# Second MLP of a three-part kernel: its sums move from GpSimd to VectorE, products are chained in PSUM, stores are issued later

## The chip, the core and the metric

The kernel runs on one core of a Trainium2 chip. The metric is the device time of one execution in microseconds (us). A core has TensorE (PE in the profile; its weight loads are PEld), VectorE (DVE), ScalarE (ACT), GpSimd (POOL) and SyncE (SP), whose queue here issues nearly all DMA transfers. Each engine takes its instructions in order; semaphores tie the engines to one another.

## The reference

The computation has three parts in a row: an attention between 512 tokens and 32 state rows for 8 x 8 heads, a first MLP with a quadratic gate, and a second MLP with a leaky slope. Both MLPs take rows of 512 through 2048 channels back to 512.

```python
def _moe_ref(x, w_in, w_out):
    h = x @ w_in
    g = np.where(h >= 1, h, np.where(h <= -1, 0.0, (h + 1) ** 2 / 4))
    return g @ w_out

def _moe2_ref(x, w_in, w_out, alpha):
    h = x @ w_in
    g = np.maximum(h, 0.0) + alpha * np.minimum(h, 0.0)
    return g @ w_out

def reference(...):
    attn_out = _attn_ref(x, state)                 # (8, 8, 544, 64)
    x = attn_out.transpose(0, 2, 1, 3).reshape(4352, 512)
    x = _moe_ref(x, ...)
    return _moe2_ref(x, ...)                       # (4352, 512)
```

The weights come as 64-bit floats; the kernel decodes them on the chip.

## The kernel before

Every f32 operand of a product is split into a high half (fp32r, rounded by ScalarE: `hi_`, L73) and a low half, the difference (`lo_`, L76, a two-operand subtraction, on VectorE unless said otherwise). A product takes three matmuls: high x high, high x low, low x high.

*First MLP and attention* (0 to 723 us). Its steps are numbered by token block t and channel block f (`gi(t, f)`); the table `side` adds other work to a step: the weights of the second MLP are decoded there, w_in in about 255 to 453 us, w_out in 464 to 670 us. For w_out the sums that the second MLP needs are made at once: `w2_sums` on GpSimd, then `w2_put`, 56 of them (8 blocks of 256 channels x 7), each a high and a low half of 128 x 256 and a store to `w2d`. For w_in the decoded halves are stored to `wid` and loaded again later.

*Second MLP* (723 to 1441 us). It is a 2 x 2 block product done with seven products instead of eight, in both layers. The tokens are cut into five supersteps s, each with two halves of 448, 448, 448, 416, 416 columns. In a superstep:

- The first layer has 56 units `h_item`: for each weight block q (0 to 7) the products p in the order 0, 1, 3 (of the q before), 5, 2 (of the q before), 4, 6. A unit is six matmuls (L757) against the input halves xh, xl. Bank A collects p 0, 5, 6, 3, bank B p 1, bank E p 4 and 2. `h_after` makes the results: ScalarE copies the bank (p, u2, u3; L783, L788, L790), VectorE adds (`plus`, L779: c11, c22, c12), ScalarE takes the negative part m (L764) and VectorE multiplies it by alpha and adds (`slope`, L766). One result, m10, has no addition.
- `g_comb` (L805) combines the four results of a q for the products of the second layer: combination 3 in the first layer, 2, 4 and 1 in the first 24 units of the second layer. All are on GpSimd.
- The second layer has 56 units `o_item` (m = 8 i + k, product PO[i] in the order 0, 1, 5, 6, 4, 3, 2). A unit is six matmuls (L830), three for each half j of 256 output columns, into a bank accB for j. `o_split` makes the halves gs of a unit three units ahead. After k = 7 `o_after` copies product 0 (ScalarE) or adds (VectorE, L843), and `out_put` transposes (L867) into a tile ot and lists its stores, of 128-byte rows.
- Beside the second layer the inputs of the next superstep are combined and split (`x_comb`, L720; `x_split`, whose second low half xl is on GpSimd), every fourth unit from m = 10.
- Superstep 0 also makes the w_in sums in its first layer: `wr_get` loads, `w1_sums` (GpSimd), `w1_put` (halves and a store to `w1d`); it uses these tiles, later supersteps load wu from `w1d` (L738).

`second` writes all this in one order. Loads of weights (wu for the first layer, wv of 256 KB for the second, L743) are put on SP's queue six units ahead; before each unit one listed store (L887) is put on the same queue. Tiles of 128 x 512 come from the pool U, of 128 x 1024 (gs, inputs xr) from V; a tile is used again when its readers are done. A scheduler then fixes each engine's order when the program is built.

Of the kernel before, what the change touches and what calls it, by code (L numbers as in the profile page):

```python
# [34 lines left out]
ROWS = S + NS  # L35
# [5 lines left out]
def kernel_body(ctx: ExitStack, tc: tile.TileContext, x, state, w1i, w1o, w2i, w2o, alpha, out):  # L41
    nc = tc.nc
    up = ctx.enter_context(tc.tile_pool(name="up", bufs=80))
    vp = ctx.enter_context(tc.tile_pool(name="vp", bufs=10))
# [51 lines left out]
    wid = dp.tile([8, 2, 128, 512], F32, name="wid")  # L96
# [545 lines left out]
    def w2i_store(j, kh):  # L642
        ld.dma_start(out=wid[j, kh], in_=G.pop(("dec", ("w2i", j, kh))))

    def wr_get(q):

        for kh in range(2):
            t = U(f"wr{q}{kh}")
            ld.dma_start(out=t, in_=wid[q, kh])
            WR[q, kh] = t  # L650
# [7 lines left out]
    def four_sums(key, a11, a12, a21, a22, view):  # L658


        sa, sb = U(f"sa{key}"), U(f"sb{key}")
        s1, s2, s3, s4 = [view(t[:, h * 256:(h + 1) * 256]) for t in (sa, sb) for h in range(2)]
        for o, a, b, op in ((s1, a21, a22, ALU.add), (s2, s1, a11, ALU.subtract),
                            (s3, a11, a21, ALU.subtract), (s4, a12, s2, ALU.subtract)):
            pool.tensor_tensor(out=o, in0=a, in1=b, op=op)
        return {0: a11, 1: a12, 2: s4, 3: a22, 4: s1, 5: s2, 6: s3}

    def put(src, name, view, dst):
        t = U(name, F32R)
        h, l = t[:, :256], t[:, 256:]  # L670
        hi_(view(h), src)
        yield
        lo_(view(l), src, view(h))
        ld.dma_start(out=dst, in_=t.bitcast(F32))
        return t

    def w1_sums(q):
        r0, r1 = [parts(WR.pop((q, kh))) for kh in range(2)]
        WS[q] = four_sums(f"a{q}", r0[:, :, 0], r1[:, :, 0], r0[:, :, 1], r1[:, :, 1],
                          lambda t: t.rearrange("p (k c) -> p k c", k=2))  # L680

    def w1_put(q, *ps):
        for p in ps:
            t = yield from put(WS[q].pop(p), f"wu{q}{p}", lambda t: t.rearrange("p (k c) -> p k c", k=2), w1d[q, p])
            WU[0, q, p] = t
            yield

    def w2_sums(q):
        r0, r1 = [G.pop(("dec", ("w2o", 2 * q + e))) for e in range(2)]
        WS["o", q] = four_sums(f"o{q}", r0[:, :256], r1[:, :256], r0[:, 256:], r1[:, 256:], lambda t: t)  # L690

    def w2_put(q, *ps):
        for p in ps:
            yield from put(WS["o", q].pop(p), f"wo{q}{p}", lambda t: t, w2d[q, p])
# [26 lines left out]

    def x_split(s, p):
# [3 lines left out]
        for kk in range(2):  # L726
# [3 lines left out]
            lo_(l, r, h, pool if kk else dve)  # L730
# [37 lines left out]
    def h_after(s, q, p):  # L768
# [26 lines left out]
        elif p == 2:  # L795
            h = plus("c12", E, GT.pop((q, "u2")))
            slope(s, q, 0, 1, h, h)
            g_comb(q, 3)

    def g_comb(q, m):  # L800

        b11, b21, b12, b22 = [GR[q, e, tk] for tk in range(2) for e in range(2)]
        x, y, op = {3: (b22, b12, ALU.subtract), 2: (b12, b11, ALU.add),
                    4: (b21, b11, ALU.subtract), 1: (b22, b11, ALU.subtract)}[m]
        pool.tensor_tensor(out={3: b12, 2: b11, 4: b21, 1: b11}[m], in0=x, in1=y, op=op)  # L805

# [11 lines left out]
    def o_item(s, i, k):  # L818
        w = wof(s)
        p = PO[i]  # L820
        gh, gl = GS.pop((i, k))
        wt = WB.pop((s, i, k))
        wh, wl = wt[:, :256], wt[:, 256:]
        for j in range(2):
            if k == 0 and p != 2:
                OA["E" if p == 4 else p, j] = acc_ps(f"accB{s}{p}{j}")
            ps = OA["E" if p in (2, 4) else p, j][:, :w]
            js = slice(j * 128, (j + 1) * 128)
            for n, (a, b) in enumerate(((wh, gh), (wh, gl), (wl, gh))):
                pe.matmul(ps, a[:, js], b, start=(p != 2 and k == 0 and n == 0), stop=(k == 7 and n == 2),  # L830
                          skip_group_check=True)
        if k == 7:
            for j in range(2):
                o_after(s, p, j)

    def o_after(s, p, j):

        w = wof(s)
        ps = OA["E" if p in (2, 4) else p, j][:, :w]

        def plus(name, b):
            o = OC[name, j] = U(f"{name}{s}{j}")[:, :w]
# [3 lines left out]
        if p == 0:  # L846
            o = OC["p0", j] = U(f"op0{s}{j}")[:, :w]
            act.copy(o, ps)
        elif p == 1:
            out_put(s, 0, j, 0, plus("c11", OC["p0", j]))  # L850
        elif p == 5:
            plus("u2", OC.pop(("p0", j)))
        elif p == 6:
            plus("u3", OC["u2", j])
        elif p == 4:
            out_put(s, 1, j, 1, plus("c22", OC["u3", j]))
        elif p == 3:
            out_put(s, 1, j, 0, plus("c21", OC.pop(("u3", j))))
# [3 lines left out]
    def out_put(s, oh, j, tk, c):  # L862
# [3 lines left out]
        t = U(f"ot{s}{oh}{j}{tk}")[:, :w]  # L866
        dve.transpose(out=t, in_=c)  # L867
        g = 2 * oh + j
        c0, end = BASE[s] + tk * w, BASE[s] + (tk + 1) * w
        first = c0  # L870
        while c0 < end:
            b, r0 = divmod(c0, S)
            if b < NB:
                n = min(end, (b + 1) * S) - c0
                dst = out[b * ROWS + r0:b * ROWS + r0 + n, :].rearrange("(b i) (g j) -> g i b j", i=32, j=32)
            else:
                n = end - c0
                dst = out.rearrange("(b r) (g j) -> g r b j", r=ROWS, j=32)[:, S:, r0 // 32:(r0 + n) // 32]
            for a in range(4):
                src = t[32 * a:32 * a + 32, c0 - first:c0 - first + n].rearrange("p (b j) -> p b j", j=32)  # L880
                OS.append((dst[4 * g + a], src))
            c0 += n

    def out_store(n):
        for _ in range(min(n, len(OS))):
            dst, src = OS.pop(0)
            ld.dma_start(out=dst, in_=src)  # L887


    def second():  # L890
# [4 lines left out]
        for s in range(NSUP):  # L895
            os = [("o", s, i, k) for i in range(7) for k in range(8)]
            hs = [("h", s, q, p) for q, p in LS]
            ev += hs[:-2]
            ev += [os[0], os[1], hs[-2], os[2], os[3], hs[-1]] + os[4:]
        loads = [e for e in ev if e[0] == "o" or e[1]]  # L900
        nl = 0
        at_load = {e: n for n, e in enumerate(loads)}
        for n, (kind, s, a, b) in enumerate(ev):
            out_store(1)
# [235 lines left out]
```

## Time and profile before

| | us |
|---|---|
| runs, not profiled | 1458.29, 1454.10, 1453.76 (median 1454.1) |
| profiled execution | 1451.19 |
| its span, first to last instruction | 1449.4 |
| TensorE busy | 1390.5 (96%) |
| VectorE busy | 1082.6 (75%) |
| ScalarE busy | 841.7 (58%) |
| GpSimd busy | 352.9 (24%) |
| mean granted clock of TensorE | 0.987 of full |

Busy time says how long an engine had an instruction under way. Matmuls are pipelined, so several short gaps of TensorE don't show in its busy time; they show in the spacing of matmuls in a window. A row of a timeline gives in brackets how long the engine had been idle and what released it. The profile's lines are those of the listing above.

### The profile page before, as it was taken

The page shows a single profiled execution, that of the slowest core. Times are in us where ns is not written, and L with a number is a line of the kernel's source. Part 1 is how long each engine was busy: PE and PEld are TensorE (multiplying, and loading weights), DVE is VectorE, ACT ScalarE, POOL GpSimd, SP SyncE. Part 2 cuts the span into 40 slices and gives each one's busy share as a digit, 9 for nine tenths or more (in the row PEclk, how much of TensorE's full clock was granted, in tenths as well). Part 3 has the DMA queues.
Part 4 walks back from the last instruction along what each step waited for, and adds up shares of the span by engine and source line. Part 5 has one row for each costly group of instructions (what it writes and reads, how often), then busy time and mean ns, then how long its engine had stood idle before and what let it go on. Part 6 is the DMA issues. An engine that isn't in the chain of part 4 may idle for free. (4 is left out here: it accounts for less than half of the span.)

```text
span 1449.4 us, 20876 instructions
## 1 busy us (share of the span) xinstructions
PE 1390.5 (96%) x6596; PEld 1197.4 (83%) x6596; DVE 1082.6 (75%) x1765; ACT 841.7 (58%) x1628; POOL 352.9 (24%) x318
## 2 busy tenths in 40 slices
PE   6799999999999999999999899999999999899997
PEld 5466688888888888888987899888988899899987
DVE  6878685868787999784698884788477857885774
ACT  5566677777776777775565453445344434454542
POOL 1000001121100121110345820371136213711350
PEclk9999999999999999999999999999999999999999
DMA  5998316878744454677376479727983799389846
GB/s 198 310 311 301 118 51 159 226 220 231 218 136 141 153 190 167 208 235 236 139 256 230 145 249 297 251 97 229 286 278 114 222 281 317 118 254 280 303 118 177
DMA packets 267869, 306.01 MB, mean 211 GB/s; under 512 B 126704, under 2 KB 141040, under 8 KB 267760
## 3 DMA queue, kind: packets, MB, share of 16 engines
q1 hardware_dynamic: 228768, 287.13, 61.7%
q0 software_dynamic: 33280, 8.51, 3.2%
q10 hardware_dynamic: 5712, 9.05, 1.7%
q8 instruction: 53, 0.87, 0.2%
q14 instruction: 56, 0.46, 0.1%
HBM read 227.42 MB, written 76.55 MB: 210 GB/s over the span
## 5 line engine op out<-in xcount | busy, mean ns | idle before, releaser
L830 PE MATMUL accB<-gs,wv 128*128 128x448 f32 (+1 forms) x1680 | 347.8, 368 | 21.2 <-DMA wv<-w2d 13.7
L830 PEld LDWEIGHTS accB<-gs,wv 128*128 128x128 f32 x1680 | 322.2, 193 | 44.4 <-issue 14.3
L757 PE MATMUL hB<-xh,wu 128*128 128x448 f32 (+1 forms) x1120 | 323.5, 364 | 10.4 <-ACT u L788 4.5
L757 PEld LDWEIGHTS hB<-xh,wu 128*128 128x128 f32 x1120 | 210.7, 189 | 33.4 <-ACT u L788 6.3
L805 POOL TENSOR_TENSOR c<-c,c 128x448 f32<-128x448 f32 (+1 forms) x120 | 157.0, 1323 | 276.0 <-DVE c L766 188.0
L757 PE MATMUL hB<-xl,wu 128*128 128x448 f32 (+1 forms) x560 | 201.8, 360 | 0.0
L76 DVE TENSOR_TENSOR gs<-c,gs 128x448 fp32r<-128x448 f32 (+1 forms) x200 | 164.4, 851 | 29.3 <-ACT gs L73 28.2
L73 ACT CAST gs<-c 128x448 fp32r<-128x448 f32 (+1 forms) x200 | 109.7, 556 | 126.5 <-PE accB L830 99.2
L764 ACT ACTIVATE m<-c 128x448 f32<-128x448 f32 (+1 forms) x120 | 68.1, 568 | 120.7 <-DVE c L779 120.7
L766 DVE SCALAR_TENSOR_TENSOR c<-m,beta_sb,c 128x448 f32<-128x448 f32 (+1 forms) x120 | 90.5, 754 | 60.6 <-ACT m L764 60.0
L582 DVE SCALAR_TENSOR_TENSOR g<-y,hA 128x512 f32<-128x512 f32 (+1 forms) x144 | 94.0, 653 | 51.6 <-ACT y L580 51.1
L579 ACT ACTIVATE y<-hA 128x512 f32<-128x512 f32 (+1 forms) x144 | 82.5, 573 | 71.8 <-PE hA L84 71.7
L76 DVE TENSOR_TENSOR gl<-g,gh 128x512 fp32r<-128x512 f32 (+1 forms) x128 | 93.0, 726 | 35.1 <-ACT gh L73 33.1
L757 PEld LDWEIGHTS hB<-xl,wu 128*128 128x128 f32 x560 | 105.6, 189 | 5.0
L73 ACT CAST gh<-g 128x512 fp32r<-128x512 f32 (+1 forms) x128 | 75.7, 591 | 25.4 <-DVE g L582 23.9
L580 ACT ACTIVATE y<-y 128x512 f32<-128x512 f32 (+1 forms) x144 | 87.6, 608 | 4.3
L779 DVE TENSOR_TENSOR c<-hB,u 128x448 f32<-128x448 f32 (+1 forms) x80 | 48.5, 606 | 47.5 <-ACT u L790 41.3
L76 DVE TENSOR_TENSOR gs<-m,gs 128x448 fp32r<-128x448 f32 (+1 forms) x80 | 72.2, 920 | 12.6 <-ACT gs L73 11.6
L76 POOL TENSOR_TENSOR xl<-xr,xh 128x448 fp32r<-128x448 f32 (+1 forms) x35 | 41.9, 1201 | 162.9 <-ACT xh L73 148.1
L606 PE MATMUL accA<-g,wf_w1o 128*128 128x512 f32 x128 | 60.5, 605 | 4.6 <-DVE wf_w1o L399 4.6
L494 ACT COPY vgo<-vgp 128x512 f32<-128x512 f32 x64 | 37.3, 587 | 43.6 <-PE vgp L84 22.4
L113 POOL TENSOR_TENSOR bdf<-stT,mask 128x512 f32<-128x512 f32 x7 | 9.4, 1342 | 213.5 <-PE accA L614 108.6
(964 smaller groups left out, 2941.3 us busy)
## 6 DMA issues: line engine op xcount, KB each, us to landing
wv<-w2d SPq DMA_DIRECT2D x280, 256.0 KB
wu<-w1d SPq DMA_DIRECT2D x224, 256.0 KB
vd<-vgo SPq DMA_DIRECT2D x64, 256.0 KB
x<-in_x_dram SPq DMA_DIRECT2D x30, 512.0 KB
vr<-vd SPq DMA_DIRECT2D x56, 256.0 KB
w2d<-wo SPq DMA_DIRECT2D x56, 256.0 KB
w1d<-wu SPq DMA_DIRECT2D x56, 256.0 KB
wr_wi<-in_moe_w_in_dram SPq DMA_DIRECT2D x16, 512.0 KB
```

What stands on the lines that cost most here:

```text
L73: act.copy(h, raw)
L76: (eng or dve).tensor_tensor(out=l, in0=raw, in1=h.bitcast(F32), op=ALU.subtract)
L579: act.activation(out=y[:, :n], in_=ps, func=AF.Relu, bias=0.5, scale=0.5)
L580: act.activation(out=y[:, :n], in_=y[:, :n], func=AF.Square)
L582: dve.scalar_tensor_tensor(out=g[:, :n], in0=y[:, :n], scalar=1.0, in1=ps, op0=ALU.min, op1=ALU.max)
L606: pe.matmul(ACC[k], w[:, k * 128:(k + 1) * 128], g, start=(f == 0), stop=(f == NF - 1))
L757: pe.matmul(ps, a[:, kk], b, start=(new and m == 0), stop=(m == 5), skip_group_check=True)
L764: act.activation(out=m, in_=h, func=AF.Relu, scale=-1.0)
L766: dve.scalar_tensor_tensor(out=g, in0=m, scalar=beta_sb[:, f:f + 1], in1=h, op0=ALU.mult, op1=ALU.add)
L779: dve.tensor_tensor(out=o, in0=a, in1=b, op=ALU.add)
L805: pool.tensor_tensor(out={3: b12, 2: b11, 4: b21, 1: b11}[m], in0=x, in1=y, op=op)
L830: pe.matmul(ps, a[:, js], b, start=(p != 2 and k == 0 and n == 0), stop=(k == 7 and n == 2), skip_group_check=True)
```

## The change

The work on GpSimd in the second MLP goes to VectorE: combinations 3 and 2 right behind the first layer's results, combination 4 in the first layer for k 0 to 3 and at m 8 to 11 for the others, combination 1 at m 23 to 30 (now written to the third result's tile); and all xl. The halves of product 0 are made in the first layer, as are the first four of product 1; the others five units ahead. Products 0, 5, 6 and 3 are chained in one bank: the sums p0 + p5 and so on form in PSUM, ScalarE copies them where another product needs them, and p3 is transposed from PSUM. A unit of the second layer is now one j with two k. The last four units of a superstep alternate with the first four of the next. A tile ot (from V) holds both j, its rows in DRAM are 256 bytes, and a store is issued at least six units after it was listed, at the very end on SP's and ScalarE's queues in turn. The w_in sums are made in the first MLP's steps, right after decoding, and superstep 0 loads wu as the others do. Pool U has 72 tiles instead of 80, V 14 instead of 10.

```diff
-    up = ctx.enter_context(tc.tile_pool(name="up", bufs=80))
-    vp = ctx.enter_context(tc.tile_pool(name="vp", bufs=10))
+    up = ctx.enter_context(tc.tile_pool(name="up", bufs=72))
+    vp = ctx.enter_context(tc.tile_pool(name="vp", bufs=14))
...
+    XAT = [11, 13, 18, 20, 22, 33, 35, 37, 42, 44, 46]
...
-            lo_(l, r, h, pool if kk else dve)
+            lo_(l, r, h)
...
             g_comb(q, 3)
+            g_comb(q, 2)
...
-        pool.tensor_tensor(out={3: b12, 2: b11, 4: b21, 1: b11}[m], in0=x, in1=y, op=op)
+        x, y, o, op = {3: (b22, b12, b12, ALU.subtract), 2: (b12, b11, b11, ALU.add),
+                       4: (b21, b11, b21, ALU.subtract), 1: (b22, b11, b12, ALU.subtract)}[m]
+        dve.tensor_tensor(out=o, in0=x, in1=y, op=op)
...
-    def o_item(s, i, k):
+    def o_item(s, i, j, ks):
         w = wof(s)
         p = PO[i]
-        gh, gl = GS.pop((i, k))
-        wt = WB.pop((s, i, k))
-        wh, wl = wt[:, :256], wt[:, 256:]
-        for j in range(2):
-            if k == 0 and p != 2:
-                OA["E" if p == 4 else p, j] = acc_ps(f"accB{s}{p}{j}")
-            ps = OA["E" if p in (2, 4) else p, j][:, :w]
-            js = slice(j * 128, (j + 1) * 128)
+        new = p in (0, 1, 4)
+        bank = {0: "A", 5: "A", 6: "A", 3: "A", 1: "B", 4: "E", 2: "E"}[p]
+        js = slice(j * 128, (j + 1) * 128)
+        for k in ks:
+            if k == 0 and new:
+                OA[bank, j] = acc_ps(f"accB{s}{p}{j}")
+            ps = OA[bank, j][:, :w]
+            gh, gl = GS[i, k]
+            wt = WB[s, i, k]
+            wh, wl = wt[:, :256], wt[:, 256:]
             for n, (a, b) in enumerate(((wh, gh), (wh, gl), (wl, gh))):
-                pe.matmul(ps, a[:, js], b, start=(p != 2 and k == 0 and n == 0), stop=(k == 7 and n == 2),
+                pe.matmul(ps, a[:, js], b, start=(new and k == 0 and n == 0), stop=(k == 7 and n == 2),
                           skip_group_check=True)
+            if j:
+                del GS[i, k], WB[s, i, k]
         if k == 7:
-            for j in range(2):
-                o_after(s, p, j)
-    def o_after(s, p, j):
+            o_after(s, p, j, ps)
...
-        if p == 0:
-            o = OC["p0", j] = U(f"op0{s}{j}")[:, :w]
+        if p in (0, 5, 6):
+            o = OC[{0: "p0", 5: "u2", 6: "u3"}[p], j] = U(f"o{p}{s}{j}")[:, :w]
             act.copy(o, ps)
         elif p == 1:
-            out_put(s, 0, j, 0, plus("c11", OC["p0", j]))
-        elif p == 5:
-            plus("u2", OC.pop(("p0", j)))
-        elif p == 6:
-            plus("u3", OC["u2", j])
+            out_put(s, 0, j, 0, plus("c11", OC.pop(("p0", j))))
         elif p == 4:
-            out_put(s, 1, j, 1, plus("c22", OC["u3", j]))
+            out_put(s, 1, j, 1, plus("c22", OC.pop(("u3", j))))
         elif p == 3:
-            out_put(s, 1, j, 0, plus("c21", OC.pop(("u3", j))))
+            out_put(s, 1, j, 0, ps)
         elif p == 2:
             out_put(s, 0, j, 1, plus("c12", OC.pop(("u2", j))))
...
+        if j == 0:
+            OC["t", oh, tk] = V(f"ot{s}{oh}{tk}")[:, :2 * w].rearrange("p (b u c) -> p b u c", u=2, c=32)
+        t = OC["t", oh, tk]
+        dve.transpose(out=t[:, :, j, :], in_=c)
+        if j == 0:
+            return
...
+                OS.append((G["unit"], dst[4 * oh + a], src))
...
     def out_store(n):
-        for _ in range(min(n, len(OS))):
-            dst, src = OS.pop(0)
-            ld.dma_start(out=dst, in_=src)
+        while OS and OS[0][0] + 6 <= n:
+            _, dst, src = OS.pop(0)
+            (ld if len(OS) % 2 or n < END else act).dma_start(out=dst, in_=src)
+            if n < END:
+                return
+    END = 10 ** 6
...
-            ev += [os[0], os[1], hs[-2], os[2], os[3], hs[-1]] + os[4:]
...
+            if s:
+                ev += [hs[0], back[0], hs[1], back[1], hs[2], back[2], hs[3], back[3]]
+            ev += hs[4 if s else 0:-2]
+            back = os[-4:]
+            ev += [os[0], os[1], hs[-2], os[2], os[3], hs[-1]] + os[4:52 if s + 1 < NSUP else 56]
...
-                if s + 1 < NSUP and a == 4 and b in (0, 1, 5, 4):
-                    xr_load(s + 1, *{0: (0, 0), 1: (1, 0), 5: (0, 1), 4: (1, 1)}[b])
-                if (a, b) == (7, 6):
-                    o_split(s, 0, 0)
-                    o_split(s, 0, 1)
-                    o_split(s, 0, 2)
+                if b == 3:
+                    o_split(s, 0, a)
+                if b == 6 and a in (1, 3, 4, 6):
+                    k = (a - 1) // 2 + a // 4
+                    o_split(s, 1, k)
+                    g_comb(k, 4)
             else:
                 m = 8 * a + b
-                if m + 3 < 56:
-                    o_split(s, *divmod(m + 3, 8))
-                if a in (0, 1, 2):
-                    g_comb(b, (2, 4, 1)[a])
-                o_item(s, a, b)
-                if s + 1 < NSUP and m >= 10 and (m - 10) % 4 == 0 and (m - 10) // 4 < len(XSTEPS):
-                    fn, arg = XSTEPS[(m - 10) // 4]
+                if 12 <= m + 5 < 56:
+                    o_split(s, *divmod(m + 5, 8))
+                if 8 <= m < 12:
+                    g_comb(m - 4, 4)
+                if 23 <= m < 31:
+                    g_comb(m - 23, 1)
+                if s + 1 < NSUP and 4 <= m < 8:
+                    xr_load(s + 1, m % 2, m // 6)
+                o_item(s, a, b % 4 // 2, [b // 4 * 4 + b % 2 * 2 + k for k in range(2)])
+                if s + 1 < NSUP and m in XAT:
+                    fn, arg = XSTEPS[XAT.index(m)]
                     fn(s + 1, arg)
-        out_store(len(OS))
+        out_store(END + 10)
...
         if key[0] == "w2i":
-            at(o + 4, w2i_store, *key[1:])
+            at(o + 1, w2i_take, *key[1:])
+            if key[2]:
+                at(o + 1, w1_sums, key[1])
+                at(o + 2, w1_put, key[1], 0, 1, 3)
+                at(o + 3, w1_put, key[1], 4, 5)
+                at(o + 4, w1_put, key[1], 6, 2)
...
-    at(gi(8, 4), wr_get, 0)
...
+    at(gi(8, 12), pre_load)
```

The scheduler's order shows the moves. On SP's queue before, in the second layer of superstep 1, this stands around the end of i = 2 (the digits of wv are s, i, k of the unit, those of ot are s, oh, j, tk of an output tile):

```order
L743 DMA wv124_10138<-w2d_91 128x512
L743 DMA wv125_10151<-w2d_91 128x512
L887 DMA out_0_dram<-ot1000_10165 32x4x32 x3
L743 DMA wv126_10172<-w2d_91 128x512
L743 DMA wv127_10187<-w2d_91 128x512
L743 DMA wv130_10200<-w2d_91 128x512
L887 DMA out_0_dram<-ot1000_10165 32x4x32
L887 DMA out_0_dram<-ot1000_10165 32x10x32
```

and in the changed kernel, at the same place:

```order
L736 DMA wv125_10187<-w2d_90 128x512
L736 DMA wv126_10189<-w2d_90 128x512
L736 DMA wv127_10203<-w2d_90 128x512
L736 DMA wv130_10223<-w2d_90 128x512
L881 DMA out_0_dram<-ot100_10173 32x4x64 x2
L736 DMA wv131_10242<-w2d_90 128x512
L736 DMA wv132_10244<-w2d_90 128x512
L736 DMA wv133_10255<-w2d_90 128x512
L881 DMA out_0_dram<-ot100_10173 32x4x64 x2
```

The first stores of the superstep's first output stood behind the load of m = 21 (i = 2, k = 5), three pieces at once; they now stand behind that of m = 24, and later pieces, each of both halves j, follow among later loads.

On VectorE, in the first layer of superstep 2, one round of additions (L779) and multiply-adds (L766), here between q = 5 and 6, was (c222_5 is result 22 of superstep 2, q = 5; hB a bank, u and p its copies, m a negative part):

```order
L779 TENSOR_TENSOR c222_5_11247<-hB254_11230,u32_5_11245 128x448
L766 SCALAR_TENSOR_TENSOR c222_5_11247<-m2511_11249,beta_sb_78,c222_5_11247 128x448
L779 TENSOR_TENSOR c112_6_11272<-hB261_11265,p02_6_11261 128x448
L766 SCALAR_TENSOR_TENSOR c112_6_11272<-m2600_11274,beta_sb_78,c112_6_11272 128x448
L766 SCALAR_TENSOR_TENSOR m2510_11285<-m2510_11285,beta_sb_78,hB250_11170 128x448
L779 TENSOR_TENSOR c122_5_11306<-hB254_11230,u22_5_11212 128x448
L766 SCALAR_TENSOR_TENSOR c122_5_11306<-m2501_11308,beta_sb_78,c122_5_11306 128x448
L779 TENSOR_TENSOR c222_6_11331<-hB264_11314,u32_6_11329 128x448
```

It now reads (additions L772, multiply-adds L759, combinations L799, low halves L76):

```order
L772 TENSOR_TENSOR c222_5_11250<-hB254_11233,u32_5_11248 128x448
L799 TENSOR_TENSOR c112_4_11095<-c122_4_11224,c112_4_11095 128x448
L759 SCALAR_TENSOR_TENSOR c222_5_11250<-m2511_11252,beta_sb_78,c222_5_11250 128x448
L772 TENSOR_TENSOR c112_6_11275<-hB261_11268,p02_6_11264 128x448
L759 SCALAR_TENSOR_TENSOR c112_6_11275<-m2600_11277,beta_sb_78,c112_6_11275 128x448
L759 SCALAR_TENSOR_TENSOR m2510_11288<-m2510_11288,beta_sb_78,hB250_11169 128x448
L76 TENSOR_TENSOR gs206_11385<-c112_6_11275,gs206_11385 128x448
L772 TENSOR_TENSOR c122_5_11312<-hB254_11233,u22_5_11214 128x448
L759 SCALAR_TENSOR_TENSOR c122_5_11312<-m2501_11314,beta_sb_78,c122_5_11312 128x448
L799 TENSOR_TENSOR c122_5_11312<-c222_5_11250,c122_5_11312 128x448
L799 TENSOR_TENSOR c112_5_11187<-c122_5_11312,c112_5_11187 128x448
L772 TENSOR_TENSOR c222_6_11338<-hB264_11321,u32_6_11336 128x448
```

A combination of the q before now stands between the first addition and its multiply-add; a low half and two more combinations have come behind multiply-adds; the order of the others is the same.

## Rows read from the trace of the kernel before

**Rows 1.** Windows, five supersteps: bounds, length, busy (count), clock, DMA; first, fourth, sum.
```profile
723.00:873.00 150.00, 143.91 (x675) 125.67 (x674) 127.58 (x190) 81.35 (x178) 72.30 (x63) 0.99 0.65 222
...
1169.30:1306.10 136.80, 130.04 (x674) 126.03 (x673) 100.03 (x144) 63.39 (x128) 48.42 (x39) 0.99 0.77 240
...
sum 718.50, PE 686.84 PEld 635.54 DVE 527.06 ACT 336.65 POOL 263.83; mean PE 137.37 PEld 127.11 DVE 105.41 ACT 67.33 POOL 52.77
```

**Rows 2.** Windows, part of a second layer at 448 columns without a wait.
```profile
1132.00:1168.00 36.00, 36.00 (x178) 33.19 (x178) 27.20 (x46) 18.60 (x36) 5.59 (x5) 1.00 0.78 228
```

**Rows 3.** Chain that ended last, one piece at 416 columns: start, us, what, count.
```profile
1328.90 40.59 PE hB L757 x216
```

**Rows 4.** Waits of PE: instruction, releaser, us in total, times, longest.
```profile
PE accB L830 <- DMA wv<-w2d: 13.7, 5, 3.6
PE accB L830 <- DVE gs L76: 7.4, 4, 1.9
PE hB L757 <- ACT u L788: 4.5, 3, 1.8
```

**Rows 5.** Windows, first layers of supersteps 0 and 2.
```profile
723.20:804.10 80.90, 78.44 (x363) 66.06 (x362) 69.57 (x114) 48.09 (x115) 38.66 (x39) 1.00 0.71 257
1023.10:1098.80 75.70, 73.64 (x361) 67.35 (x360) 47.15 (x69) 33.63 (x65) 19.44 (x15) 1.00 0.92 290
```

**Rows 6.** Timeline of PE, superstep 1, second layer: start, us, what, [idle before].
```profile
968.12 8.91 PE L830 MATMUL accB<-gs,wv 128*128 128x448 f32 x35 [1.91 <-DVE gs L76]
979.38 5.84 PE L830 MATMUL accB<-gs,wv 128*128 128x448 f32 x20 [2.34 <-DMA wv<-w2d]
```

**Rows 7.** Timeline of DVE over the same stretch.
```profile
965.51 2.02 DVE L720 TENSOR_TENSOR xr<-xr,xr 128x896 f32<-128x896 f32 x1 [2.17 <-POOL xl L76]
967.45 5.60 DVE L76 TENSOR_TENSOR gs<-c,gs 128x448 fp32r<-128x448 f32 x5
974.48 0.63 DVE L867 STREAM_TRANSPOSE ot<-c 128x448 f32<-128x448 f32 x1
976.07 0.63 DVE L867 STREAM_TRANSPOSE ot<-c 128x448 f32<-128x448 f32 x1
```

**Rows 8.** Waits of the SP queue, the longest one.
```profile
SPq L887 <- DVE ot L867: 170.5, 11, 28.3
```

**Rows 9.** Windows, seven stretches at half clock after 723 us: first, sum.
```profile
969.10:972.40 3.30, 3.30 (x11) 2.90 (x10) 3.30 (x3) 1.05 (x2) 3.30 (x3) 0.50 0.00 0
...
sum 25.80, PE 24.40 PEld 22.35 DVE 20.66 ACT 6.06 POOL 15.27; mean PE 3.49 PEld 3.19 DVE 2.95 ACT 0.87 POOL 2.18
```

**Rows 10.** Timeline of DVE, part of a round of a first layer.
```profile
1073.80 0.63 DVE L76 TENSOR_TENSOR gs<-c,gs 128x448 fp32r<-128x448 f32 x1
1074.35 0.62 DVE L779 TENSOR_TENSOR c<-hB,u 128x448 f32<-128x448 f32 x1
1075.61 0.69 DVE L766 SCALAR_TENSOR_TENSOR c<-m,beta_sb,c 128x448 f32<-128x448 f32 x1 [0.65 <-ACT m L764]
```

**Rows 11.** Groups of DVE: what, count, busy us, mean ns, idle before.
```profile
L76 DVE TENSOR_TENSOR gs<-c,gs 128x448 fp32r<-128x448 f32 (+1 forms) x200 | 164.4, 851 | 29.3 <-ACT gs L73 28.2
L76 DVE TENSOR_TENSOR gs<-m,gs 128x448 fp32r<-128x448 f32 (+1 forms) x80 | 72.2, 920 | 12.6 <-ACT gs L73 11.6
L76 DVE TENSOR_TENSOR wo<-wf_w2o,wo 128x256 fp32r<-128x256 f32 x24 | 9.4, 422 | 1.2 <-ACT wo L73 1.2
```

**Rows 12.** Groups of POOL.
```profile
L805 POOL TENSOR_TENSOR c<-c,c 128x448 f32<-128x448 f32 (+1 forms) x120 | 157.0, 1323 | 276.0 <-DVE c L766 188.0 <-PE hB L757 23.7 <-DMA wu<-w1d 21.1
L76 POOL TENSOR_TENSOR xl<-xr,xh 128x448 fp32r<-128x448 f32 (+1 forms) x35 | 41.9, 1201 | 162.9 <-ACT xh L73 148.1 <-DMA out_dram<-ot 7.8 <-DMA wv<-w2d 4.9
```

**Rows 13.** Windows of the first MLP: decoding of w_in, then of w_out.
```profile
255.00:453.00 198.00, 198.00 (x917) 164.32 (x916) 155.42 (x277) 146.11 (x268) 25.27 (x30) 1.00 0.71 205
464.00:670.00 206.00, 205.68 (x934) 169.88 (x934) 171.10 (x321) 154.42 (x297) 31.69 (x34) 1.00 0.57 190
```

**Rows 14.** Timeline of the end, the SP queue.
```profile
1435.87 10.89 SPq L887 DMA_DIRECT2D out_dram<-ot  x22
```

More of the change, by code (lines that the diff above doesn't have):

```diff
@@ L640, in src_w2p, with w2i_take @@
         return w2i[kh * 256:(kh + 1) * 256, j * 256:(j + 1) * 256].rearrange("(k p) c -> p k c", k=2)
[L642 to L650, printed above, removed]
+    def w2i_take(j, kh):
+        WR[j, kh] = G.pop(("dec", ("w2i", j, kh)))
     def parts(t):
@@ L664, in four_sums @@
                             (s3, a11, a21, ALU.subtract), (s4, a12, s2, ALU.subtract)):
-            pool.tensor_tensor(out=o, in0=a, in1=b, op=op)
+            eng.tensor_tensor(out=o, in0=a, in1=b, op=op)
         return {0: a11, 1: a12, 2: s4, 3: a22, 4: s1, 5: s2, 6: s3}
@@ L689, in w2_sums @@
         r0, r1 = [G.pop(("dec", ("w2o", 2 * q + e))) for e in range(2)]
-        WS["o", q] = four_sums(f"o{q}", r0[:, :256], r1[:, :256], r0[:, 256:], r1[:, 256:], lambda t: t)
+        WS["o", q] = four_sums(f"o{q}", r0[:, :256], r1[:, :256], r0[:, 256:], r1[:, 256:], lambda t: t, pool)
     def w2_put(q, *ps):
         for p in ps:
-            yield from put(WS["o", q].pop(p), f"wo{q}{p}", lambda t: t, w2d[q, p])
+            yield from put(WS["o", q].pop(p).rearrange("p (a j c) -> p a j c", a=4, j=2), f"wo{q}{p}",
+                           lambda t: t.rearrange("p (j a c) -> p a j c", a=4, j=2), w2d[q, p])
             yield
@@ L895, in second @@
         for s in range(NSUP):
-            os = [("o", s, i, k) for i in range(7) for k in range(8)]
+            os = [("o", s, n // 8, n % 8) for n in range(56)]
             hs = [("h", s, q, p) for q, p in LS]
-            ev += hs[:-2]
-            ev += [os[0], os[1], hs[-2], os[2], os[3], hs[-1]] + os[4:]
-        loads = [e for e in ev if e[0] == "o" or e[1]]
-        nl = 0
-        at_load = {e: n for n, e in enumerate(loads)}
-        for n, (kind, s, a, b) in enumerate(ev):
-            out_store(1)
-            while nl < len(loads) and nl <= at_load.get(ev[min(n + ahead, len(ev) - 1)], -1):
-                (w2_get if loads[nl][0] == "o" else w1_get)(*loads[nl][1:])
+            if s:
[3 more added lines that the diff above has]
+            ev += [os[0], os[1], hs[-2], os[2], os[3], hs[-1]] + os[4:52 if s + 1 < NSUP else 56]
+        loads, need = [], []
+        for n, (kind, s, a, b) in enumerate(ev):
+            if kind == "h":
+                loads.append((w1_get, s, a, b))
+                need.append(n)
+            elif kind == "o" and b % 4 < 2:
+                for k in range(2):
+                    loads.append((w2_get, s, a, b // 4 * 4 + b % 4 * 2 + k))
+                    need.append(n + k)
+        nl = 6
+        for n, (kind, s, a, b) in enumerate(ev):
+            G["unit"] = n
+            out_store(n)
+            while nl < len(loads) and need[nl] <= n + ahead:
+                fn, *arg = loads[nl]
+                fn(*arg)
                 nl += 1
```

53 lines of the change are left out of this document (16 added, 37 removed).

## The prediction

> **What bounds the kernel now.** First the windows by superstep: the second MLP takes 718.5 us in five supersteps [rows 1]. A stretch of TensorE without a wait gives its floor: 36.00 us for 177 to 178 matmuls of 448 columns, 0.2034 each [rows 2], and 216 of 416 columns in 40.59 us, 0.188 each [rows 3]. A superstep has 672 matmuls, so the floor is 2016 x 0.2034 + 1344 x 0.188 = 662.8 us, and 55.7 us are lost: 13.3 in superstep 0 (150.0 - 136.7), 10.5 in superstep 3 (136.8 - 126.3) [rows 1].
>
> Then where they go. In the windows of the first layers (336 matmuls and the 24 of the second layer that stand among them: 360 x 0.2034 = 73.2), superstep 0, which also makes the w_in sums, loses 80.9 - 73.2 = 7.7 us, superstep 2 only 2.5 [rows 5]. If the others do as superstep 2, the first layers lose 7.7 + 4 x 2.5 = 18, the second layers 38. The list of waits names TensorE's longest: 13.7 us on weight loads, 7.4 on VectorE's low halves, 4.5 on a ScalarE copy [rows 4]. The timeline shows the first two just after a second layer starts: 1.91 us behind gs, 2.34 behind wv [rows 6]. VectorE's timeline over the same stretch explains them. At 965.51 it had waited 2.17 us for GpSimd's xl, so the gs behind it came late. Then five gs took 5.60 us, 1.12 each, where one alone takes 0.63 [rows 7, 10], because GpSimd was at work (in 969.1 to 972.4 it was busy all the time [rows 9]). So the transposes come at 974.48 and 976.07, and the stores that need them hold SP's queue (170.5 us in 11 waits, up to 28.3 [rows 8]); the weight loads behind them in that queue are late. Behind such waits TensorE gets a granted clock of 0.50: seven stretches, 25.8 us, in which half, 12.9, is lost [rows 9]. The listed waits (25.6) and the clock (12.9) give 38.5; the other 17 are smaller gaps and restarts.
>
> **The change part by part.**
> *Combinations and xl to VectorE.* GpSimd's operations last 1323 and 1201 ns [rows 12]; on VectorE, alone, two-operand sums of this shape take 0.62 to 0.63 [rows 10], so 160 + 35 operations add about 195 x 0.6 = 117 us. Against that the 280 gs that now last 164.4 + 72.2 = 236.6 us [rows 11] fall to 280 x 0.61 (0.63 at 448, some 0.58 at 416) = 171, minus 66; the 30 additions that the chained banks save and the 49 puts of superstep 0 that leave (0.6 and 0.5 each) take 42 more. Other two-operand sums gain too; I leave them as reserve. VectorE's 527 us [rows 1] stay within some 10. So the gain isn't less work but its place: it leaves the start of the second layer.
>
> *Second layer.* The xl wait and the stretched gs go, low halves are made five units ahead instead of three, product 0's before the layer starts, and a store is issued at least six units after its transpose, when it holds no load. Both causes of the waits named above end; the half clock behind them goes too. The loads keep their lead of six units, and the rows of the changed SP order show the store three loads later. What is late next: the ScalarE copies of the chained banks at the end of products 0, 5 and 6; between 5 and 6, and so in the tightest place, 6 matmuls of the other half j (1.2 us) leave time for one. I take 1 us lost per superstep, bounds 0 and 5.6 (what superstep 0 loses there now, 13.3 - 7.7).
>
> *First layer.* VectorE's round per weight block q is now three pairs, 1.26 us from addition to the multiply-add (0.65 of it waiting for ScalarE) and 0.69 for that, and one more multiply-add: 3 x 1.95 + 0.69 = 6.54 us [rows 10], beside TensorE's 42 x 0.2034 = 8.54 [rows 2]. Added are two combinations, one and a half gs and half a combination: 4 x 0.62 = 2.48. If none falls into the waits the round is 9.02; if all three waits are filled, 7.1. The changed order puts a combination between an addition and its multiply-add now and then, not always. So no slack is left: between the 2.5 us that a first layer with slack loses and the 7.7 of superstep 0 [rows 5] I take 4.5. It is the largest open size of the sum; bounds 2.5 and 11 (third rival).
>
> The Trainium skill ("Perfetto Trace Analysis", Optimizing Scalar/DVE Operations) speaks against taking work back from GpSimd: where VectorE is saturated, offloading may make sense, though the two share an SBUF read port and it may not help. By its first half VectorE would become the bound, which is the second rival; the gs of 1.12 us beside GpSimd [rows 7] bear out the second half more. Its page "SBUF — State Buffer" (Who interferes with whom) says that a VectorE instruction with two SBUF inputs and a reading GpSimd instruction block each other whole. By that a combination costs VectorE its reading time on either engine and the total falls by the removed 42 only, to 485; the rows give about 530 to 540 without the reserve. Both keep the first layers near their bound.
>
> *w_in sums at decoding.* 56 puts at 0.42 us on VectorE [rows 11] enter the w_in window: 155.42 + 23.6 = 179 of 198 us, 90% [rows 13]. The w_out window already holds 56 such puts and GpSimd's sums at 171 of 206, 83%, and TensorE loses 0.3 there [rows 13]. The round trip of the decoded halves through DRAM (32 transfers of 256 KB) leaves SP; 56 stores move from the second MLP to here. I take 2 us lost, bounds 0 and 15 (puts 0.42, stretched by GpSimd as gs were, 0.63 x 1.4, bring VectorE to 100% and the first layer of the MLP behind). Superstep 0 loses its puts; it now counts like the others.
>
> *End.* After the last matmuls SP issues 22 stores one after the other, 10.89 us [rows 14]. Half as many on two queues, but each waits for both halves j: minus 2, bounds minus 5 and plus 1.
>
> **The sum.** Retained per superstep 4.5 + 1 = 5.5, together 27.5 of 55.7: minus 28.2. With plus 2 and minus 2: 1451.2 - 28.2 = 1423.0. The profiled execution is 2.9 below the median of 1454.1, so 1425.9, rounded to 1426.
>
> **The rivals.**
> *VectorE becomes the bound of the first layers.* No wait is filled, the round is 9.02, 8 x 0.48 = 3.8 us more on top of the 4.5: 8.3 + 1 per superstep, 46.5 retained. 1451.2 - 9.2 + 2.9 = 1445. For it: superstep 0 lost 7.7 with VectorE busy for 69.57 of 80.90; 47.15 of 75.70 in superstep 2 [rows 5] plus 8 x 2.48 = 67 would be 88%. Against: that VectorE time was partly stretched by GpSimd.
> *The first MLP pays for the sums.* Plus 14 instead of 2: 1438. For it: 90% beside GpSimd's sums; against: the w_out window.
> *Slower: the additions wait for ScalarE in a ring.* ScalarE's queue is in order, and the copy that frees bank A for the next product stands behind a negative part m that waits for VectorE's addition. If VectorE's added work comes before that addition, the copy is late, TensorE waits, and the next addition too. With nothing filled and each of three waits 0.3 longer the round is 9.9: 8 x 1.4 = 11 per layer, one half-clock stretch per superstep (12.9 / 7 = 1.8) and 1: 69 retained, 1451.2 + 13 + 2.9 = 1467. It decides from a round of about 9.5 on: (9.5 - 8.54) x 8 = 7.7, with 1.8 + 1 about the 11.1 retained now. For it: 4.5 us of waits on that copy already [rows 4]. Against: 2 us of slack per round now, and some combinations may stand where VectorE waits.
> *The change doesn't do what it says:* gs stay at 0.85 without GpSimd, VectorE's total rises by 110, and the second layer keeps its lags: about 1454.
>
> **How the numbers follow.** Forecast 0.67; VectorE bound 0.13; first MLP 0.09; slower 0.07; no shortening 0.04. The forecast's own range is 12 to 42 retained: 1410 to 1440. The range goes on to the VectorE bound and down for a first layer without loss: 1406 to 1448; it leaves out the last two cases and a little of the others. A measurement of this kernel tells 0.3%, 4.4 us, from no change: faster is below 1449.7. Forecast, bound and first MLP lie there (0.89, minus 0.02 for their tails); same 0.05 from the last case and tails; slower 0.08.
>
> **What would show it.** Right: no wait of VectorE on GpSimd and none of SP on ot; gs near 0.61 us; no wait of TensorE on wv; second layers within 1 us of 336 matmuls at their spacing; half clock in fewer than seven stretches. The first layers decide: VectorE's idle time there on ScalarE's m, and TensorE's waits on u, should come to 4 or 5 us each. Wrong: first layers 8 us or more above their floor, TensorE waiting on u or p copies in every round, or a w_in window in which TensorE drops below 196 of 198. If w2d loads still come late with SP free, the transfers themselves were the cause and the second layers keep their loss.

## The result: 1413 us, more won than forecast, in one place, and part of it paid back in another

The changed kernel takes 1413.05 us (median; 1410.63 to 1418.24) against 1453.93: ratio 0.972, 95% interval 0.968 to 0.976. The forecast was 1426 (1406 to 1448). So the direction and the range held, and 41 us were won where 28 were forecast. The profiled execution is 1411.49 us, its span 1409.7.

First the second MLP as one window, before and now, from its first matmul to the end of the last (columns as in [rows 1]), then TensorE's waits in it, which answer to [rows 4], and the groups of gs, which answer to [rows 11].

```profile
723.20:1441.30 718.10, 686.44 (x3361) 635.34 (x3360) 526.75 (x750) 336.65 (x676) 263.83 (x212) 0.98 0.72 227
734.30:1403.20 668.90, 667.43 (x3398) 633.10 (x3396) 493.83 (x863) 329.07 (x651) 0.00 (x0) 1.00 0.74 241
```

```profile
PE hB L750 <- ACT u L783: 0.6, 1, 0.6
PE accB L825 <- ACT o L843: 0.5, 1, 0.5
PE hB L750 <- ACT p L776: 0.2, 1, 0.2
```

```profile
L76 DVE TENSOR_TENSOR gs<-c,gs 128x448 fp32r<-128x448 f32 (+1 forms) x200 | 114.8, 602 | 7.1 <-ACT gs L73 6.4
L76 DVE TENSOR_TENSOR gs<-m,gs 128x448 fp32r<-128x448 f32 (+1 forms) x80 | 46.9, 601 | 16.8 <-ACT gs L73 16.8
```

TensorE's listed waits fell from 25.6 to 1.3 us, no stretch of this window is at half clock, gs fell from 851 and 920 to 602 ns. Before, the second MLP took 718.1 us (723.2 to 1441.3). Its present 668.9 hold a piece of the first MLP: the row of its output matmuls (L613) behind the second MLP's first matmul is

```profile
734.20:739.60 5.40, 4.48 (x36) 4.59 (x36) 1.00 0.24 92
```

36 matmuls of 256 columns, 0.12 us apart, 4.3 us. So the second MLP itself takes 664.6, 1.8 above its floor of 662.8, and the first MLP ends as if at 738.6 instead of 723.2. The books of the two profiled executions: second MLP minus 53.5, first MLP plus 15.4, end (8.1 to 6.5 us after the last matmul) minus 1.6: minus 39.7.

The first MLP pays mostly in the w_in window, the same work that was 198.00 us before [rows 13] (columns as there):

```profile
253.70:464.60 210.90, 202.70 (x916) 162.69 (x915) 173.88 (x320) 157.93 (x311) 50.51 (x58) 1.00 0.76 229
475.80:685.40 209.60, 206.74 (x934) 169.40 (x933) 172.56 (x327) 155.21 (x304) 35.13 (x37) 1.00 0.53 180
```

12.9 us there and 3.6 in the w_out window.

The first layer of superstep 2 (336 matmuls, 24 of the second layer and 24 of the one before: 384 x 0.2034 = 78.1) loses 0.3 us, and VectorE is busy 68% of it; the window, and a piece of VectorE's timeline:

```profile
1007.50:1085.90 78.40, 78.31 (x386) 71.92 (x385) 53.47 (x88) 35.34 (x68) 0.00 (x0) 1.00 0.77 240
```

```profile
1045.37 0.62 DVE L772 TENSOR_TENSOR c<-hB,u 128x448 f32<-128x448 f32 x1
1045.91 1.28 DVE L799 TENSOR_TENSOR c<-c,c 128x448 f32<-128x448 f32 x2
1047.11 0.68 DVE L759 SCALAR_TENSOR_TENSOR c<-m,beta_sb,c 128x448 f32<-128x448 f32 x1
```

Two combinations stand between an addition and its multiply-add, which then has no wait in brackets: here the 0.65 us that VectorE idled [rows 10] are used. Most multiply-adds of this layer still wait for ScalarE's negative part m, as VectorE's waits in the first layer of superstep 2 say, before and now (the total, how often, the longest):

```profile
DVE c L766 <- ACT m L764: 13.0, 20, 0.7
DVE c L759 <- ACT m L757: 9.7, 15, 0.6
```

### The profile page after: what moved, and what is told of

Its sections match the earlier page's. It is cut to its first block, busy times and chain, and to the rows that moved or that the text cites. A ratio compares the mean times of both kernels' runs of the same rounds, so it can differ in the third digit from the quotient of the medians.

```text
span 1409.7 us, 20512 instructions
## 1 busy us (share of the span) xinstructions
PE 1373.5 (97%) x6596; PEld 1190.5 (84%) x6596; DVE 1065.9 (76%) x1930; ACT 846.1 (60%) x1648; POOL 103.0 (7%) x123
## 4 chain that ended last, share of the span: by engine, by line
PE 81%; DVE 6%; DMA 5%; ACT 5%; issue 1%; ACTq 0%; SPq 0%; DVEq 0%
PE accB L825 23%; PE hB L750 23%; PE accA L613 15%; PE hA L84 10%; PE accA L605 4%; DMA vr<-vd 3%; PE vgp L84 2%; DMA vd<-vgo 1%; PE sr L84 1%; ACT oA L624 1%; DMA w1d<-wu 1%; PE sc L84 1%; DVE g L581 1%; PE vdp L84 1%; DVE xt L142 1%
## 5 line engine op out<-in xcount | busy, mean ns | idle before, releaser
L825 PE MATMUL accB<-gs,wv 128*128 128x448 f32 (+1 forms) x1680 | 334.3, 359 | 0.5 <-ACT o L843 0.5
L825 PEld LDWEIGHTS accB<-gs,wv 128*128 128x128 f32 x1680 | 314.8, 188 | 16.2 <-ACT o L843 0.8
L750 PE MATMUL hB<-xh,wu 128*128 128x448 f32 (+1 forms) x1120 | 317.0, 360 | 1.0 <-ACT u L783 0.6
L76 DVE TENSOR_TENSOR gs<-c,gs 128x448 fp32r<-128x448 f32 (+1 forms) x200 | 114.8, 602 | 7.1 <-ACT gs L73 6.4
L759 DVE SCALAR_TENSOR_TENSOR c<-m,beta_sb,c 128x448 f32<-128x448 f32 (+1 forms) x120 | 80.4, 670 | 48.2 <-ACT m L757 45.6
L76 DVE TENSOR_TENSOR gl<-g,gh 128x512 fp32r<-128x512 f32 (+1 forms) x128 | 91.2, 713 | 31.6 <-ACT gh L73 29.6
L799 DVE TENSOR_TENSOR c<-c,c 128x448 f32<-128x448 f32 (+1 forms) x120 | 71.4, 608 | 2.0
L772 DVE TENSOR_TENSOR c<-hB,u 128x448 f32<-128x448 f32 (+1 forms) x80 | 48.5, 606 | 25.2 <-PE hB L750 13.4
L76 DVE TENSOR_TENSOR gs<-m,gs 128x448 fp32r<-128x448 f32 (+1 forms) x80 | 46.9, 601 | 16.8 <-ACT gs L73 16.8
L73 ACT CAST gs<-m 128x448 fp32r<-128x448 f32 (+1 forms) x80 | 43.1, 555 | 24.3 <-PE accB L825 20.0
L605 PEld LDWEIGHTS accA<-g,wf_w1o 128*128 128x128 f32 x128 | 24.1, 190 | 25.5 <-issue 18.8
```

The costliest lines, as they stand in the source:

```text
L73: act.copy(h, raw)
L76: (eng or dve).tensor_tensor(out=l, in0=raw, in1=h.bitcast(F32), op=ALU.subtract)
L605: pe.matmul(ACC[k], w[:, k * 128:(k + 1) * 128], g, start=(f == 0), stop=(f == NF - 1))
L750: pe.matmul(ps, a[:, kk], b, start=(new and m == 0), stop=(m == 5), skip_group_check=True)
L759: dve.scalar_tensor_tensor(out=g, in0=m, scalar=beta_sb[:, f:f + 1], in1=h, op0=ALU.mult, op1=ALU.add)
L799: dve.tensor_tensor(out=o, in0=x, in1=y, op=op)
```

## The experiments

All ratios are to the kernel before, with 95% intervals. "Second MLP" is its window, less 4.3 us where the 36 matmuls stand in it.

**e3: only the engine.** The kernel before, with

```diff
-            lo_(l, r, h, pool if kk else dve)
+            lo_(l, r, h)
...
-        pool.tensor_tensor(out={3: b12, 2: b11, 4: b21, 1: b11}[m], in0=x, in1=y, op=op)
+        dve.tensor_tensor(out={3: b12, 2: b11, 4: b21, 1: b11}[m], in0=x, in1=y, op=op)
```

> The kernel before with combinations and xl on VectorE, each at its old place; stores, chains and w_in sums as before. Theory (engine and place both count): gs fall from 850 to about 610 ns, the waits on xl go, but VectorE's second layer is still full and the stores still stand in front of the loads: 1425 to 1440 us. Rival 1 (GpSimd's contention is all): 1415 or less. Rival 2 (VectorE was the bound and gets longer): 1460 or more.

1404.15 us, 0.967 (0.965 to 0.969): two lines do better than the whole change, and rival 1 holds. The second MLP's window, and SP's longest wait:

```profile
724.50:1393.50 669.00, 666.07 (x3362) 628.16 (x3360) 529.75 (x938) 337.81 (x676) 20.98 (x24) 1.00 0.77 244
```

```profile
SPq L887 <- DVE ot L867: 136.0, 10, 20.5
```

SP's queue is still held by stores, 136.0 us in all and up to 20.5 (170.5 and 28.3 before [rows 8]), and no wait on wv is left: holds of that length did no harm, and the longer ones went with VectorE's lateness. VectorE does 188 more operations in this window and is busy for 529.75 us, against 526.75 before: what the added ones take, the others win back. By the groups of e3 the 188 take 112 us (an estimate, at some 0.6 each), so the other 750 took about 417: some 109 us less than beside the GpSimd operations, 0.58 for each of the 188.

**e5: GpSimd at work for nobody.** e3 plus, at the old places,

```diff
+            if kk:
+                pool.tensor_tensor(out=idle[:, :w], in0=h.bitcast(F32), in1=l.bitcast(F32), op=ALU.add)
...
             g_comb(q, 3)
+            pool.tensor_tensor(out=idle[:, :w], in0=GR[q, 0, 1], in1=GR[q, 1, 1], op=ALU.add)
...
                     g_comb(b, (2, 4, 1)[a])
+                    h, l = GS[divmod(m + 3, 8)]
+                    pool.tensor_tensor(out=idle[:, :wof(s)], in0=h.bitcast(F32), in1=l.bitcast(F32), op=ALU.add)
```

(U has 79 tiles, to make room.)

> The kernel of e3 (before, with combinations and xl on VectorE) plus as many GpSimd operations of the same size at the places of the old ones (160 beside the combinations, 35 beside xl), which read two tiles that others have made and write a tile that nobody reads. Theory (a GpSimd operation stretches VectorE's two-operand operations beside it): gs rise from 610 to 800 ns or more, VectorE has both its own work and the stretch, and at least 30 of the 49 us won in the second MLP are lost again: 1434 us or more. Rival (what cost time was that GpSimd's results came late): nobody waits for these operations, 1404 to 1410 us.

1513.54 us, 1.043 (1.041 to 1.045). No result of these operations is used, and the second MLP is 108.5 us longer than in e3. The window, TensorE's first waits, and ScalarE's on GpSimd:

```profile
723.90:1501.40 777.50, 706.08 (x3362) 636.71 (x3360) 646.34 (x938) 333.86 (x676) 287.81 (x212) 0.97 0.66 210
```

```profile
PE accB L834 <- DVE gs L76: 40.5, 35, 3.0
PE accB L834 <- DMA wv<-w2d: 19.0, 10, 10.8
ACT gs L73 <- POOL idle L937: 125.1, 80, 9.3
```

VectorE's 938 instructions are the same as in e3 and take 646.34 instead of 529.75 us: 116.6 us for the 188 GpSimd operations in this window, 0.62 each. So the stretch of the theory is there, without any late result. The rival is less clearly out than the time suggests, for it isn't so that nobody waits: an added operation reads a tile gs, the tile can't be used again before the operation is done, and ScalarE's next high halves wait for that, 80 times. The 108.5 us are the stretch and these waits together; how they divide stays open. In the kernel before, too, there is some of both: VectorE's and ScalarE's listed waits on GpSimd in the second MLP come to 22 us there. The waits on wv are back, and stores now hold SP's queue for up to 37.9 us.

The Trainium skill ("SBUF — State Buffer", Who interferes with whom) says that a VectorE instruction with two SBUF inputs and a reading GpSimd instruction block each other whole. The trace agrees: while GpSimd does seven operations without a pause in e5 (971.4 to 981.7 us, 1.47 each), VectorE's start about 1.49 us apart, one for each of GpSimd's, where in a pause of GpSimd just before (965.65 to 967.26) they start 0.54 apart. e3's unchanged busy time fits as well, and so does the changed kernel's: 493.83 us lie nearer to the 485 that the prediction worked out by this rule than to its 530 to 540.

**e6: GpSimd in the new places.** The changed kernel with

```diff
-        dve.tensor_tensor(out=o, in0=x, in1=y, op=op)
+        pool.tensor_tensor(out=o, in0=x, in1=y, op=op)
```

> The changed kernel with its combinations on GpSimd again, at their new places in both layers; xl stays on VectorE. Theory (the engine is what matters): gs above 700 ns, second MLP 690 us or longer against 669, 1432 us or more. Rival (the new places, the longer lead and the late stores matter as much): second MLP under 680 us, 1424 or less.

1422.35 us, 0.980 (0.977 to 0.982); gs at 779 and 690 ns, so the stretch is there, but the second MLP is 677.1 - 4.3 = 672.8 us. The rival holds. With e3: taking GpSimd out, or the rest of the change (the new places, the longer lead, the chains, the later stores and the early w_in sums, with xl on VectorE), each cures most of the second MLP's loss by itself. They don't add up: 55.3 us of loss became 6.2 in e3, 10.0 in e6, 1.8 with both.

**e4 and e12: the stores alone.** e4 is the kernel before with

```diff
-        for _ in range(min(n, len(OS))):
+        while OS and OS[0][0] + 6 <= n:
```

and one store per unit; e12 is the changed kernel with

```diff
-        while OS and OS[0][0] + 6 <= n:
+        while OS and OS[0][0] <= n:
```

> The kernel before with the stores issued six units after they are listed, one per unit, all else as before. Theory (the held queue costs its waits on wv and the half clock behind them): waits of TensorE on wv 13.7 to about 0, 15 to 20 us gained, 1434 to 1440 us. Rival (the transposes' lateness only shows at the next thing): under 6 us gained, 1448 or more.

> The changed kernel with each store issued from the unit that lists it instead of six units later, still one per unit. Theory (after e3: the held queue hurts only while VectorE is late): no wait of TensorE on wv over 1 us in the second MLP, within 4 us of 1413. Rival (the late issue is what keeps the loads free): waits on wv as before, 1422 us or more.

e4: 1465.43 us, 1.008 (1.005 to 1.011), TensorE's waits on wv 15.4 us in place of 13.7 and on ScalarE's copy p 8.6 in place of 1.7. The theory is missed; the rival's bound of 1448 or more holds, but it named no loss, and why there is one stays open. It is a weak test, for on SP's queue of superstep 1 the first three stores still come behind the same 18 loads in a row. e12: 1421.14 us, 0.977 (0.976 to 0.979), between the two expectations. Its second MLP is 673.1 us, 8.5 longer, and no wait on wv is listed; the longest is

```profile
PE accB L825 <- ACT o L843: 4.9, 4, 1.6
```

So late issue is worth some us beside the chained banks, and not by freeing the loads; how, stays open.

**e1, e2, e7: where the first MLP's time goes.** e1 is the changed kernel with the w_in part undone; e7 the kernel before with that part alone; e2 the changed kernel with the old pools:

```diff
-    up = ctx.enter_context(tc.tile_pool(name="up", bufs=72))
-    vp = ctx.enter_context(tc.tile_pool(name="vp", bufs=14))
+    up = ctx.enter_context(tc.tile_pool(name="up", bufs=80))
+    vp = ctx.enter_context(tc.tile_pool(name="vp", bufs=10))
```

> The changed kernel with its w_in part undone: halves of w_in go through DRAM again, sums and puts are in superstep 0's first layer. Theory (the early sums cost the first MLP about 14 us, the rest of the change gives some 50): the first MLP ends at 722 to 724 us again, superstep 0's first layer loses 5 to 8 us as before; about 1404 to 1407 us. Rival 1 (the smaller tile pool U, 72 for 80, costs the first MLP its time): the first MLP still ends at 730 or later, 1415 or more. Rival 2 (superstep 0 pays the sums in full, since VectorE has no slack left there): loss of 12 or more in superstep 0, 1411 or more.

> The changed kernel with the pools of before (U 80, V 10). Theory (work on VectorE, ScalarE and GpSimd is what the first MLP pays for): the w_in window stays 208 us or longer against 198; the second MLP, with four fewer wide tiles, loses more than now. Rival (tiles of U that wait for their store are what the first MLP pays for): the window comes down to 200 us or less and the second MLP begins before 726.

> The kernel before with the w_in sums made at decoding as in the changed one, pools U 80 and V 10 as before, all else as before. Theory (the sums themselves load the first MLP): the second MLP begins at 733 to 739 us instead of 723, superstep 0 gets 5 to 8 us shorter: 1456 to 1464 us. Rival (the first MLP's loss comes from the smaller pool U, which this kernel doesn't have): it begins before 728, 1446 to 1450 us.

e1: 1412.26 us, 0.972 (0.970 to 0.974), which misses its theory's 1404 to 1407; e2: 1423.61, 0.980 (0.977 to 0.982); e7: 1465.79, 1.010 (1.008 to 1.012), a little beyond its theory. The w_in window, matched by its matmuls, in e7 and e1:

```profile
254.60:465.20 210.60, 202.71 (x916) 164.52 (x916) 171.99 (x321) 157.35 (x311) 54.63 (x58) 0.99 0.75 225
```

```profile
252.90:456.60 203.70, 199.18 (x916) 164.01 (x915) 153.98 (x278) 146.19 (x269) 25.55 (x30) 1.00 0.70 197
```

In e2 it is 209.3. The early sums cost it 11.3 to 12.6 us with U 80 (e2, e7) and 7.2 with U 72 (210.9 - 203.7); the new pools without them cost 5.7 (e1). Over the whole first MLP the pools look otherwise. It ends 15.4 us later than before in the changed kernel, 21.6 in e2, 20.6 in e7, and 4.4 in e1, where the second MLP begins at 727.55. So the new pools cost about 4 us without the early sums and save about 6 with them. (e6 and e12, whose edits don't touch the first MLP, end it 2.7 us later than the changed kernel; differences of that size between these single profiles say little.) Made late, the sums cost the second MLP what they save the first: it takes 676.4 us in e1, 11.8 more. So early or late, they cost about the same in the changed kernel. In the kernel before, early sums lose 20.6 us in the first MLP (second MLP from 739.5, with 4.3 us of the first behind that) and win 6.7 in the second (711.4 for 718.1).

**e9 and e10: which part of the sums.** e9 gives the four sums of each w_in block to VectorE. e10 leaves out the puts' low halves and stores the high half in both places, so that the low part of w_in is missing from its result:

```diff
-                          lambda t: t.rearrange("p (k c) -> p k c", k=2), pool)
+                          lambda t: t.rearrange("p (k c) -> p k c", k=2), dve)
```

```diff
-        lo_(l, src, h)
-        ld.dma_start(out=dst, in_=t.bitcast(F32))
+        if low:
...
+        else:
+            for c in (0, 256):
+                ld.dma_start(out=dst[:, c:c + 256], in_=t[:, :256].bitcast(F32))
```

> The changed kernel with the four sums of each w_in block (32 operations of 128 x 256) on VectorE instead of GpSimd in the first MLP. Theory (VectorE's and ScalarE's own load is what the w_in window pays for): 32 x 0.42 = 13 us more on VectorE, the window stays at 209 us or longer, 1412 to 1420 us. Rival (GpSimd's sums, which stretch VectorE beside them and stand in GpSimd's queue before the loads of ws, are the cause): the window comes down to 203 us or less, 1405 or less.

> The changed kernel without the 56 low halves of w_in's puts on VectorE in the first MLP; the high half is stored in both places, so the low part of w_in is left out of the result. Takes 24 us of VectorE work from the w_in window and the wait of the stores on it. Theory (VectorE's added work): the window comes down to 203 us or less, the second MLP begins before 728, 1405 or less. Rival (what remains, ScalarE's high halves, GpSimd's sums and the 56 stores, is enough): 208 us or more.

e9: 1418.15 us, 0.976 (0.975 to 0.978), the window 214.0, as its theory had it: with the sums on VectorE the first MLP pays no less, so GpSimd as their place isn't the cause. e10: 1421.72 us, 0.979 (0.977 to 0.980), and its window:

```profile
253.40:473.20 219.80, 206.16 (x917) 166.82 (x916) 160.09 (x277) 160.45 (x318) 48.68 (x58) 0.98 0.77 220
```

VectorE is 14 us less busy than in the changed kernel and the window 9 us longer, so nothing bears out my theory of VectorE's load. It isn't a clean test, for e10 has 56 more stores in SP's queue. What it shares with the others is ScalarE's high halves and the stores. Which of them holds the first MLP up stays open.

**e8 and e11: better versions.** e11 is e3 with

```diff
-            ld.dma_start(out=dst, in_=src)
+            (act if last and len(OS) % 2 else ld).dma_start(out=dst, in_=src)
```

where `last` is true for what is left at the very end. e8 also gives superstep 0's w_in sums (blocks q 1 to 7) to VectorE.

> The kernel of e3 with the w_in sums of superstep 0 on VectorE too (so nothing is left on GpSimd in the second MLP), and the stores left at the very end on SP's and ScalarE's queues in turn. Theory: superstep 0 comes from 139.9 to 138 us, the end is 3 to 5 us shorter: 1397 to 1401 us. Rival (VectorE has no room in superstep 0, and the stores are bounded by their last transpose): 1403 to 1406 us.

> The kernel of e3 with only the stores left at the very end on SP's and ScalarE's queues in turn. Theory: the end after the last matmul goes from 8.6 to 5 us, 1399 to 1402 us against 1404 of e3. Rival (the last transposes and the landing of the last store bound the end): 1403 to 1405 us.

e11: 1402.44 us, 0.9655 (0.964 to 0.967), the fastest of all. Its second MLP is 669.0 us as in e3, the end 6.7 instead of 8.6; the difference to e3 is too small for these runs to tell. e8: 1409.76 us, 0.971 (0.969 to 0.974), slower than e3, the other way than expected. The first layer of superstep 0 in e3, and in e8 with its only listed wait of TensorE:

```profile
724.50:801.30 76.80, 75.28 (x363) 67.03 (x362) 69.95 (x129) 47.94 (x115) 20.98 (x24) 1.00 0.75 267
```

```profile
725.50:809.10 83.60, 77.61 (x363) 66.28 (x362) 72.64 (x157) 47.63 (x115) 0.00 (x0) 1.00 0.68 244
```

```profile
PE hB L757 <- ACT u L788: 5.5, 6, 1.2
```

10.4 us lost against 3.6. That is the ring of the third rival. VectorE is hardly busier (72.64 us for 69.95), but the four sums of a block, from 746.48 us on, now stand ahead of an addition. ScalarE's negative part waits 2.27 us for that addition, its copy of the bank comes behind, and at 750.93 TensorE has waited 1.09 for the copy. In all, ScalarE waits 32.1 us for additions here, in e3 24.0. Here GpSimd, with 24 sums of half the size, was the better place.

## Why the prediction was right, and where its sizes were not

*What bounds.* Right. The two stalls at the start of each second layer had one root, VectorE late beside GpSimd; e3 makes them go, and e5 makes them grow. That VectorE is stretched there is shown; that the stretch alone, without the waits for GpSimd (the xl of the prediction among them), makes the loss is not.

*The held store queue* as a cause of its own: wrong. In e3 it is held for 136.0 us and no weight load is late. Nor do the later stores free it. The prediction has a store issued "when it holds no load"; in the changed kernel SP's longest wait is

```profile
SPq L881 <- DVE ot L860: 117.7, 15, 12.2
```

and no load is late all the same.

*Combinations and xl to VectorE.* "The gain isn't less work but its place" is half wrong. VectorE's total stays in e3 (529.75 for 526.75 us) but falls by 33 in the changed kernel, beyond the forecast's "within some 10": other two-operand operations gained as well, which the prediction had left as reserve. And e3 moves nothing in place and gains 49.1 of the 53.5 us. What was gained is that VectorE's second-layer work no longer meets GpSimd just where TensorE waits for it.

*First layer, 4.5 us retained per superstep:* the term that was mis-sized most. Measured 0.3 in superstep 2. I added 8 x 2.48, that is 32 operations, to 47.15 us; but the window holds only 19 instructions more (88 for 69), since the 12 gs that I counted as added took the place of 10, and the mean of one fell from 0.68 to 0.61 us. So VectorE was busy 53.47 of 78.40 us, not 67 of 76. That left room enough: it still waits for ScalarE's m 9.7 us of the 13.0 before, so the round was not saved by filling the waits. With 1 us for the second layer I kept 27.5 us of the loss; 1.8 was left (minus 53.5 for the forecast minus 28.2: 25.3 us more gained).

*w_in sums at decoding, plus 2:* mis-sized the other way, plus 15.4 (13.4 us more lost), just past the bound of 15 and near the second rival's 14. I took the value of the w_out window, which loses nothing with as many puts. The two windows aren't alike; in what, stays open. The new pools, which I gave no price, don't explain it: with the old ones (e2) the first MLP loses 21.6.

*End, minus 2:* measured minus 1.6.

The two misses have opposite signs: 25.3 - 13.4 - 0.4 at the end = 11.5, the forecast's error for the profiled execution (1423.0 to 1411.5). That the range held is in part luck: with the second MLP as measured and the other terms as forecast the time is 1451.2 - 53.5 + 2 - 2 + 2.9 = 1401 us, below the range's 1406. The first rival (VectorE as the bound, which the prediction once calls the second) did not occur; the second did, beside the forecast and not in its place; the third is seen in e8 alone.

*The signs.* As named for "right": no wait of VectorE on GpSimd, none of TensorE on wv, gs at 0.60, no half clock. Against them: SP still waits for ot, VectorE's idle time on m is 9.7 us in a first layer and TensorE's waits on u are 0.6 in all, where 4 or 5 each were named. And a sign of "wrong" came up: in the w_in window TensorE is busy for 202.70 of 210.90 us, 96%, below 196 of 198.

## What to carry to other kernels

Ask first for the smallest edit that takes away the root: here two lines did better than the change that also re-ordered, chained and delayed. When two cures are offered for one loss, each may do it alone, and the second then brings little but its costs (here 4.4 of 55.3 us). Work taken from a critical stretch has a price where it goes, and a neighbouring window with the same work is no proof that it is free.

## What the runs showed of the hardware

A GpSimd operation of 128 x 448 or 416 with two SBUF inputs, whose result nobody reads, cost VectorE 0.62 us (e5 against e3), as much as doing it there. Taking as many off GpSimd gave VectorE's other instructions back 0.58 us each (e3 against the kernel before, an estimate from the groups' times). A given list of VectorE instructions thus took 529.75 or 646.34 us by what GpSimd did beside it.
